# Taps of the last unit's first two tiles in two parts, and another order for the second half of the work

## The chip, the cores and the metric

One core of a Trainium2 chip. The metric is device time of the kernel in microseconds (us), the median of several executions; beside it stands one profiled execution, from which all durations come. The engines: TensorE (PE, its weight loads PEld), VectorE (DVE), ScalarE (ACT), GpSimd (POOL) and SyncE (SP, which issues loads).

## What is computed

Linear attention with a decaying state feeds a gated block:

```python
# q, k, v: (B=4, H=8, S=768, D=64)
for t in range(S):
    state = gamma * state + k[:, :, t] (outer) v[:, :, t]
    y[:, :, t] = scale * (q[:, :, t] @ state)
x = y.transpose(0, 2, 1, 3).reshape(B, S, 512)
gate = sigmoid(sum(conv_w[k] * x_shifted_by(4 - k) for k in range(5)))   # 5 taps along the sequence
out = (gate * (x @ w_val)) @ w_out
```

All inputs are float32, except the three weights of the block, which come in as float64.

## The kernel before

The sequence is cut into six chunks of 128 positions. A **unit** n (0 to 5) is one chunk with all four batches, 512 columns wide. Work on a unit comes in three kinds, which the code writes as letters of a string `WORK` (lines 60 to 64):

- `v`, a visit (`attention`, L896): the attention of one batch in one chunk, by 64x64 matmuls. It runs in two halves that TensorE may not interrupt (`hold`): `visit` (L502: outputs from the masked scores, L462; states, L446) and `rest_of_visit` (L514: outputs from the state, L462; scores of the next batch, L389). Between them ScalarE copies one column (`turn`, L512). In the last chunk the first half has no state matmuls of its own batch, and in the very last visit none at all. Afterwards VectorE masks the next scores (`mask`, L411) and writes the outputs into x (`evac`, L542); ScalarE rounds x (`round_x`, L552) and GpSimd takes the rest (`rest_x`, L557). GpSimd scales the next batch (`decay`, L378), ScalarE takes two copies of the state (`snap`, L457). A load for four batches ahead goes on SP's queue.
- `V`, a value tile (`val_tile`, L999; matmuls L680): 12 matmuls of 128x512, x times a quarter of w_val, in three passes (rounded x with both parts of the weight, rest of x with the rounded weight). With it comes `conv` (L973): the gate of that quarter, one tap on ScalarE (L662), four on VectorE (L664, each 128x512, accumulating in a PSUM tile `acc` of which there are two), and a sigmoid on ScalarE (L672). A tap reads all four batches, so the taps of a unit wait for the last visit of that unit. VectorE multiplies tile and gate (`gated`, L695).
- `O`, an output product. Units 1 to 4 use seven products of 12 matmuls of 128x256 each (`product_at`, L1067; L757), numbered 0 to 6 here, whose operands are sums and differences of quarters made on GpSimd (`g_sum`, L725; `g_low`, L742) and rounded on ScalarE (L738). Units 0 and 5 use four plain tiles (`out_tile`, L1098; L800).

Value tiles and products share two PSUM banks (`mm`): the products 0 and 2, 1 and 3, 4 and 6 share one bank each, so that bank stays taken from the first to the second of the pair. A new tile waits for the one two before it to be read out.

`WORK` gives each step a due time by adding up nominal durations. The function `plan` (L98) then orders all steps: each step gets a rank, its own due time or earlier if someone needs it earlier, and whenever an engine comes free, the ready step with the lowest rank is put next on that engine's queue, by fixed estimated durations. So the string gives an order of preference, not the order itself. The queues are in order on the chip: a step that isn't ready holds up what is queued behind it on its engine.

The last unit's end goes so: its fourth visit, evacuation, rounding, its taps, four value tiles, four output tiles, the last one in two halves.

Of the kernel before, what the change touches and what calls it, by code (L numbers as in the profile page):

```python
# [16 lines left out]
P = 128  # L17
HALF = 64
NPAIR = 4
TAPS = 5  # L20
# [24 lines left out]
TIMES = {  # L45
    "DVE": (0.69, 0.60),
    "tap": (0.76, 0.665),
    "ACT": (0.62, 0.525),
    "snap": (0.38, 0.28),
    "POOL": (1.29, 1.24),  # L50
    "decay": (1.05, 1.01),
}
# [6 lines left out]

WORK = (  # L60
    "spyzsyzsysyzwwzVVhwwvVVvOOOvOvvvVVvVVvTVOOVO"
    "VOvOvOvVvOVOOOVvOvOOVVvvOVOVOOOVVOOOvOvOvvOO"
    "OVOVVVOOOOO"
)

# [220 lines left out]
def tile_retention_gated_mlp(  # L286
# [10 lines left out]
    B, S, DM = out.shape  # L297
# [3 lines left out]
    NU = NCH  # L301
# [41 lines left out]
    def at(due, engine, cost, reads, writes, fn, *args):  # L343
        steps.append(Step(due, engine, cost, list(reads), list(writes), fn, args))
        return steps[-1]
# [6 lines left out]
    tiles, us, snaps, xs, xh, xl, decs, pos_ps = {}, {}, {}, {}, {}, {}, {0: base}, []  # L352
# [300 lines left out]
    accs, gvs, vps, ops, outs = {}, {}, {}, {}, {}  # L653
    gu, operands, banks, held = {}, {}, {}, {}

    def tap(n, m, k):
        x = xs[n][:, m]
        if k == 0:
            accs[n, m] = ps_a.tile([P, UT], F32, name="acc")
        acc = accs[n, m].rearrange("p (b t) -> p b t", t=P)  # L660
        if k == 0:
            nc.scalar.mul(acc, x[:, :, 0:P], cw_sb[:, m, 0:1])  # L662
        else:
            nc.vector.scalar_tensor_tensor(  # L664
                acc, x[:, :, k:k + P], cw_sb[:, m, k:k + 1], acc,
                op0=ALU.mult, op1=ALU.add,
            )
# [211 lines left out]
    def decay_at(t, g):  # L879
        at(t, "POOL", TIMES["decay"], ["small"], [("att", g % LB, "kn" if g < B else "vk")], decay, g)  # L880

    def scored_at(t, g):

        us_of[g] = Slot("u", 2)
        at(t, "DVE", TIMES["DVE"], [scored[g], "small"], [us_of[g]], mask, g)
        at(t + 0.01, "ACT", TIMES["snap"], ["z"], taken[g][1:], snap, g, 1)
# [9 lines left out]
    def attention(g, t):  # L896

        b, c = chunks[g]
        qk, vk = ("att", g % LB, "qk"), ("att", g % LB, "vk")
        u, y = us_of.pop(g), Slot("y", 1)  # L900
        n = 32
        if g + 1 < NG:
            decay_at(t - 0.01, g + 1)
            taken[g + 1] = [Slot("snap", 4), Slot("snap", 4)]
            at(t - 0.005, "ACT", TIMES["snap"], ["z"], taken[g + 1][0:1], snap, g + 1, 0)
            n += 16
        if c < NCH - 1:
            n += 16
        step = at(t, "PE", 1.0, [u, vk] + ([("att", (g + 1) % LB, "vk")] if g + 1 < NG else []), [y, "z"], visit, g)
        step.small = n  # L910
        step.turn = at(t + 0.5, "ACT", (0.25, 0.2), [y], ["turn"], turn, g)
        reads, writes = [qk, "turn"] + taken[g], [y]
        if g + 1 < NG:
            scored[g + 1] = Slot("sc", 1)
            reads.append(("att", (g + 1) % LB, "qk"))
            writes.append(scored[g + 1])
        step.hold = at(t + 1.0, "PE", 1.0, reads, writes, rest_of_visit, g)
        step.hold.small = 64 if g + 1 < NG else 32
        if g + 1 < NG:
            scored_at(t + 1.01, g + 1)  # L920
        if b == 0:
            xbufs[c] = Slot("x", XB)
            last = [xbufs[c - 1]] + [("x", c - 1, i) for i in range(B)]
            at(t + 0.5, "ACT", (0.25, 0.15), last, [xbufs[c]] + [("x", c, i) for i in range(B)], new_x, c)
        at(t + 1.9, "DVE", TIMES["DVE"], [y, ("dec", c % 2), xbufs[c]], [("x", c, b)], evac, g)
        if c + 1 < NCH:
            at(t + 2.4, "ACT", (0.4, 0.3), ["base", "small"], [("dec", (c + 1) % 2)], table, c + 1, b)
        split(c, b, t + 1.95)
        whole[c] = t + 2.0

    def convert(t, n):
        raw = wsts[n] if n != "cw" else "cwraw"
# [40 lines left out]
    def conv(n, m, t):  # L973
        acc = Slot("acc", 2)
        x = [xbufs[n]] + [("x", n, b) for b in range(B)]
        at(t, "ACT", (0.7, 0.62), x + ["cw"], [acc], tap, n, m, 0)
        for k in range(1, TAPS):
            at(t + 0.1 * k, "DVE", TIMES["tap"], x + ["cw"], [acc], tap, n, m, k)
        gates[n, m] = ("g", n, m)
        if m % 2 == 0:  # L980
            gslots[n, m // 2] = Slot("gate", GU)
        s = at(t + 0.5, "ACT", (0.6, 0.49), [acc], [gates[n, m]], sigmoid, n, m)
        if m % 2 == 0:
            s.writes += [gslots[n, m // 2], ("gopen", n, m // 2)]
        else:
            s.keeps.append(gslots[n, m // 2])
            s.reads.append(("gopen", n, m // 2))

    gslots, ops_of = {}, {}

    def split(n, b, t):
        if b == 0:
# [132 lines left out]
    for p, (kind, n) in enumerate(LOADS):  # L1125
        t = 0.1 * p
# [18 lines left out]
    t, whole = 6.0, {}  # L1145
# [3 lines left out]
    for what in WORK:  # L1149
        i = now[what]  # L1150
        now[what] += 1
        n, m = divmod(i, NPAIR)
# [4 lines left out]
        elif what == "s":  # L1157
            t = max(t, 6.0 + CHUNK * i)
# [27 lines left out]
        else:  # L1186
            n, m = products[i]
# [103 lines left out]
```

## Time and profile before

| | us |
|---|---|
| median of 3 runs (204.81 to 205.15) | 205.12 |
| the profiled execution | 205.91 |
| its span | 204.00 |
| TensorE busy | 195.1 (96%) |
| VectorE busy | 131.4 (64%) |
| ScalarE busy | 113.8 (56%) |
| GpSimd busy | 150.2 (74%) |

The span is the time from the first to the last recorded event; 1.91 us of the profiled execution lie around it. A visit appears as L462, L446, L462, L389 in TensorE's rows. Value matmuls (L680) and products (L757) stand between visits, partly interleaved one by one.

### The profile page before, as it was taken

Reading aid. Unit: us, or ns where it says so; the run is one execution under the profiler, and the core shown is the slowest. Engines: PE = TensorE matmul, PEld = TensorE weight load, DVE = VectorE, ACT = ScalarE, POOL = GpSimd, SP = SyncE. Lnnn points to the kernel's source line nnn. Section 1 sums busy time; section 2 is a strip of 40 time slices with the busy share of each in tenths; the row PEclk is TensorE's granted clock in tenths of the full one; section 3 lists DMA queues with packets and bytes.
Section 4 is the critical chain, followed back from the end, with each engine's and each line's share of the span. In section 5 each row is a group of like instructions: output and inputs, shape, how many; then the busy total and the mean of one; then the engine's idle time right before and its main releaser. Section 6 shows DMA issues by size and latency. Waiting matters only on the chain.

```text
span 204.0 us, 8170 instructions
## 1 busy us (share of the span) xinstructions
PE 195.1 (96%) x3640; PEld 164.3 (81%) x3640; DVE 131.4 (64%) x200; ACT 113.8 (56%) x245; POOL 150.2 (74%) x129
## 2 busy tenths in 40 slices
PE   8778999899998999999999999999999999999993
PEld 3456877778877888988988989988898998987882
DVE  1367799732878939994359995399922543999100
ACT  3476788935679468675138755247651535434221
POOL 0479999999989998999906999826995599222500
PEclk9999999999999999999999999999999999999998
DMA  6999998546846453364564472680010130220022
GB/s 199 371 416 416 408 421 297 214 180 223 286 159 249 181 209 154 111 234 141 208 177 175 140 286 82 261 274 3 3 51 0 55 109 0 103 78 28 0 103 103
DMA packets 11301, 36.25 MB, mean 178 GB/s; under 512 B 1154, under 2 KB 5634, under 8 KB 8708
## 3 DMA queue, kind: packets, MB, share of 16 engines
q1 hardware_dynamic: 5472, 29.43, 38.8%
q10 hardware_dynamic: 5796, 6.32, 9.2%
q8 instruction: 28, 0.46, 0.9%
q14 instruction: 5, 0.04, 0.1%
HBM read 29.46 MB, written 6.29 MB: 175 GB/s over the span
## 4 chain that ended last, share of the span: by engine, by line
PE 67%; DMA 4%; ACT 2%; DVE 0%; issue 0%; ACTq 0%
PE mm L680 27%; PE mm L757 20%; PE sy L462 8%; PE mm L800 6%; DMA out_dram<-o_sb 4%; PE sy L389 3%; PE z_ps L446 3%; ACT gate L672 0%; DVE top L787 0%; ACT snap L457 0%; ACT o_sb L813 0%; ACT acc L662 0%; ACT turned L512 0%; ACT gate L813 0%; ACT wst L646 0%
## 5 line engine op out<-in xcount | busy, mean ns | idle before, releaser
L664 DVE SCALAR_TENSOR_TENSOR acc<-x,cw_sb,acc 128x512 f32<-128x512 f32 x96 | 67.7, 750 | 4.4 <-ACT acc L662 3.8
L557 POOL TENSOR_TENSOR xl<-x,xh 128x512 fp32r<-128x512 f32 x24 | 31.2, 1301 | 11.2 <-ACT xh L552 11.2
L742 POOL TENSOR_TENSOR gvl<-gate,gvh 128x512 fp32r<-128x512 f32 x24 | 30.8, 1299 | 7.6 <-ACT gvh L738 7.6
L378 POOL TENSOR_TENSOR att<-att,small_sb 128x512 f32<-128x512 f32 x24 | 25.3, 1055 | 10.3 <-DMA att<-in_att_dram 10.2
L680 PE MATMUL mm<-xl,wvh 128*128 128x512 f32 x96 | 32.8, 398 | 0.0
L680 PE MATMUL mm<-xh,wvh 128*128 128x512 f32 x96 | 31.5, 405 | 0.4 <-ACT xh L552 0.4
L680 PE MATMUL mm<-xh,wvl 128*128 128x512 f32 x96 | 28.7, 397 | 0.0
L411 DVE TENSOR_TENSOR u<-sy,small_sb 128x512 f32<-128x512 f32 x20 | 13.7, 686 | 14.3 <-PE sy L389 8.9
L695 DVE TENSOR_TENSOR gate<-mm,gate 128x512 f32<-128x512 f32 x24 | 16.4, 685 | 8.9 <-PE mm L680 8.7
L672 ACT ACTIVATE gate<-acc 128x512 f32<-128x512 f32 x24 | 14.4, 603 | 13.7 <-DVE acc L664 12.2
L725 POOL TENSOR_TENSOR gate<-gate 128x512 f32<-128x512 f32 x16 | 20.6, 1293 | 0.5 <-DVE gate L695 0.4
L680 PEld LDWEIGHTS mm<-xl,wvh 128*128 128x128 f32 x96 | 17.9, 188 | 3.7
L680 PEld LDWEIGHTS mm<-xh,wvh 128*128 128x128 f32 x96 | 17.3, 188 | 4.4 <-ACT xh L552 0.6
L680 PEld LDWEIGHTS mm<-xh,wvl 128*128 128x128 f32 x96 | 17.7, 188 | 3.8
L552 ACT CAST xh<-x 128x512 fp32r<-128x512 f32 x24 | 14.8, 618 | 10.0 <-DVE x L542 9.6
L738 ACT CAST gvh<-gate 128x512 fp32r<-128x512 f32 x24 | 14.5, 620 | 9.5 <-DVE gate L695 5.3
L706 POOL TENSOR_TENSOR gvl<-gate,gvh 128x512 fp32r<-128x512 f32 x8 | 10.4, 1296 | 11.7 <-ACT gvh L702 11.7
L662 ACT ACTIVATE acc<-x,cw_sb 128x512 f32<-128x512 f32 x24 | 16.6, 694 | 3.7 <-DVE x L542 3.6
L542 DVE TENSOR_TENSOR x<-sy,dec 128x512 f32<-128x512 f32 x20 | 13.6, 682 | 7.5 <-ACT snap L457 3.2
L457 ACT COPY snap<-z_ps 128x256 f32<-128x256 f32 x40 | 14.1, 375 | 2.9 <-PE sy L462 1.7
L757 PE MATMUL mm<-wst,gvh 128*128 128x256 f32 x96 | 15.5, 282 | 0.0
L462 PEld LDWEIGHTS sy<-u,att 64*64 64x64 f32 x640 | 11.2, 134 | 5.3 <-issue 2.9
(78 smaller groups left out, 382.7 us busy)
## 6 DMA issues: line engine op xcount, KB each, us to landing
att<-in_att_dram SPq DMA_DIRECT2D x20, 1024.0 KB, 5.3
wst<-in_w_dram SPq DMA_DIRECT2D x8, 512.0 KB, 10.4
out_dram<-o_sb ACTq DMA_DIRECT2D x15, 256.0 KB, 2.9
att<-in_att_dram SPq DMA_DIRECT2D x3, 768.0 KB, 8.9
out_dram<-top ACTq DMA_DIRECT2D x8, 256.0 KB, 2.4
att<-in_att_dram SPq DMA_DIRECT2D x5, 256.0 KB, 5.5
att<-in_att_dram SPq DMA_DIRECT2D x1, 512.0 KB, 3.5
out_dram<-gate ACTq DMA_DIRECT2D x2, 128.0 KB, 1.7
```

The costliest lines, as they stand in the source:

```text
L378: nc.gpsimd.tensor_tensor(v, v, vd_sb[:, c, :].unsqueeze(2).broadcast_to([P, 8, HALF]), op=ALU.mult)
L462: nc.tensor.matmul(sy[cols, h, off:off + HALF], lhsT=lhsT, rhs=rhs, start=start, stop=True, skip_group_check=True,)
L552: nc.scalar.copy(xh[n][:, :, b], xs[n][:, :, b, HALO:])
L557: nc.gpsimd.tensor_tensor(xl[n][:, :, b], xs[n][:, :, b, HALO:], xh[n][:, :, b].bitcast(F32), op=ALU.subtract)
L662: nc.scalar.mul(acc, x[:, :, 0:P], cw_sb[:, m, 0:1])
L664: nc.vector.scalar_tensor_tensor(acc, x[:, :, k:k + P], cw_sb[:, m, k:k + 1], acc, op0=ALU.mult, op1=ALU.add,)
L680: nc.tensor.matmul(vps[n, m], lhsT=w[:, m, ct * P:(ct + 1) * P], rhs=xx[n][:, ct].rearrange("p b t -> p (b t)"), start=(i == 0), stop=(i = ...
L695: nc.vector.tensor_tensor(gv, vps.pop((n, m)), gv, op=ALU.mult)
L725: engine.tensor_tensor(block(n, k), block(n, a), block(n, b), op=getattr(ALU, op))
L738: nc.scalar.copy(g_part(n, k, 0), block(n, k))
L742: engine.tensor_tensor(low, block(n, k), operands[n, k, 0].bitcast(F32), op=ALU.subtract)
L757: nc.tensor.matmul(banks[bank][:, tt * 256:(tt + 1) * 256], lhsT=g[:, ct, tt * P:(tt + 1) * P], rhs=weight(w, part % 2)[:, ct], start=(k i ...
```

## The change

The taps of value tiles 0 and 1 of unit 5 are made in two parts. The first part covers batches 0 to 2 (384 of 512 columns) and becomes due right after the third visit of that unit; the second covers batch 3 (128 columns) and waits for the fourth. The ScalarE tap and the four VectorE taps each become two instructions, so ten instructions for these tiles become twenty. The other tiles keep whole taps. The middle line of `WORK` is another string with the same letters; the first three of its 44 letters stay. By units and batches (v4.2 is the visit of batch 2 in unit 4, V3.1 value tile 1 of unit 3, O2.5 product 5 of unit 2), from the first differing letter on, before:

```
O1.4 v3.1 O1.5 v3.2 V2.3 v3.3 O1.6 V3.0 O2.0 O2.1 O2.2 V3.1 v4.0 O2.3 v4.1 O2.4 O2.5 V3.2 V3.3 v4.2 v4.3
O2.6 V4.0 O3.0 V4.1 O3.1 O3.2 O3.3 V4.2 V4.3 O3.4 O3.5 O3.6 v5.0 O4.0 v5.1 O4.1 v5.2 v5.3
O4.2 O4.3 O4.4 V5.0 O4.5 V5.1 V5.2 V5.3 O4.6 O5.0 O5.1 O5.2 O5.3
```

and after:

```
v3.1 v3.2 O1.4 v3.3 O1.5 V2.3 V3.0 v4.0 V3.1 v4.1 O1.6 O2.0 O2.1 V3.2 O2.2 v4.2 v4.3
V3.3 O2.3 V4.0 O2.4 O2.5 V4.1 V4.2 O2.6 O3.0 O3.1 V4.3 O3.2 O3.3 O3.4 O3.5 O3.6 v5.0 O4.0 v5.1 O4.1 O4.2 O4.3 v5.2 v5.3
O4.4 V5.0 O4.5 V5.1 V5.2 V5.3 O4.6 O5.0 O5.1 O5.2 O5.3
```

```diff
--- before.py
+++ after.py
@@ -59,7 +59,7 @@
 
 WORK = (
     "spyzsyzsysyzwwzVVhwwvVVvOOOvOvvvVVvVVvTVOOVO"
-    "VOvOvOvVvOVOOOVvOvOOVVvvOVOVOOOVVOOOvOvOvvOO"
+    "VOvvvOvOVVvVvOOOVOvvVOVOOVVOOOVOOOOOvOvOOOvv"
     "OVOVVVOOOOO"
 )
 
@@ -653,11 +653,11 @@
     accs, gvs, vps, ops, outs = {}, {}, {}, {}, {}
     gu, operands, banks, held = {}, {}, {}, {}
 
-    def tap(n, m, k):
-        x = xs[n][:, m]
-        if k == 0:
+    def tap(n, m, k, b0=0, b1=B):
+        x = xs[n][:, m, b0:b1]
+        if k == 0 and b0 == 0:
             accs[n, m] = ps_a.tile([P, UT], F32, name="acc")
-        acc = accs[n, m].rearrange("p (b t) -> p b t", t=P)
+        acc = accs[n, m].rearrange("p (b t) -> p b t", t=P)[:, b0:b1]
         if k == 0:
             nc.scalar.mul(acc, x[:, :, 0:P], cw_sb[:, m, 0:1])
         else:
@@ -926,7 +926,7 @@
         if c + 1 < NCH:
             at(t + 2.4, "ACT", (0.4, 0.3), ["base", "small"], [("dec", (c + 1) % 2)], table, c + 1, b)
         split(c, b, t + 1.95)
-        whole[c] = t + 2.0
+        whole[c] = has_x[c, b] = t + 2.0
 
     def convert(t, n):
         raw = wsts[n] if n != "cw" else "cwraw"
@@ -973,9 +973,19 @@
     def conv(n, m, t):
         acc = Slot("acc", 2)
         x = [xbufs[n]] + [("x", n, b) for b in range(B)]
-        at(t, "ACT", (0.7, 0.62), x + ["cw"], [acc], tap, n, m, 0)
-        for k in range(1, TAPS):
-            at(t + 0.1 * k, "DVE", TIMES["tap"], x + ["cw"], [acc], tap, n, m, k)
+        if n == NU - 1 and m < 2:
+            t3 = min(t, has_x[n, 2] + 0.01)
+            x3, x1 = x[0:B] + ["cw"], [x[0], x[B], "cw"]
+            at(t3, "ACT", (0.56, 0.48), x3, [acc], tap, n, m, 0, 0, 3)
+            for k in range(1, TAPS):
+                at(t3 + 0.01 * k, "DVE", (0.61, 0.52), x3, [acc], tap, n, m, k, 0, 3)
+            at(t + 0.05, "ACT", (0.38, 0.3), x1, [acc], tap, n, m, 0, 3, 4)
+            for k in range(1, TAPS):
+                at(t + 0.1 * k, "DVE", (0.35, 0.26), x1, [acc], tap, n, m, k, 3, 4)
+        else:
+            at(t, "ACT", (0.7, 0.62), x + ["cw"], [acc], tap, n, m, 0)
+            for k in range(1, TAPS):
+                at(t + 0.1 * k, "DVE", TIMES["tap"], x + ["cw"], [acc], tap, n, m, k)
         gates[n, m] = ("g", n, m)
         if m % 2 == 0:
             gslots[n, m // 2] = Slot("gate", GU)
@@ -986,7 +996,7 @@
             s.keeps.append(gslots[n, m // 2])
             s.reads.append(("gopen", n, m // 2))
 
-    gslots, ops_of = {}, {}
+    gslots, ops_of, has_x = {}, {}, {}
 
     def split(n, b, t):
         if b == 0:
```

## Rows read from the trace of the kernel before

**Rows 1.** The page: busy us of each engine, share of the span.

```profile
PE 195.1 (96%) x3640; PEld 164.3 (81%) x3640; DVE 131.4 (64%) x200; ACT 113.8 (56%) x245; POOL 150.2 (74%) x129
```

**Rows 2.** Stages: length, engines' busy us, granted clock, DMA share, GB/s.

```profile
20.27:62.29 42.02, 40.89 (x951) 32.60 (x952) 28.90 (x45) 30.87 (x69) 41.44 (x36) 1.00 0.75 278
62.29:169.56 107.27, 107.09 (x2146) 94.77 (x2146) 76.16 (x116) 59.61 (x131) 87.77 (x74) 1.00 0.41 143
169.56:200.67 31.11, 30.77 (x228) 26.37 (x227) 16.85 (x26) 11.31 (x20) 9.90 (x8) 1.00 0.17 60
```

**Rows 3.** TensorE's waits after 62 us: total, times, longest.

```profile
PE sy L462 <- ACT turned L512: 0.8, 2, 0.5
```

**Rows 4.** TensorE by time, at 60.61: start, us, instructions, idle before.

```profile
58.79 1.20 PE L680 MATMUL mm<-xh,wvh 128*128 128x512 f32 x4
59.83 0.85 PE L680 MATMUL mm<-xh,wvl 128*128 128x512 f32 x3
60.61 0.69 PE L462 MATMUL sy<-u,att 64*64 64x64 f32 x32
...
62.29 0.69 PE L462 MATMUL sy<-att,snap 64*64 64x64 f32 x32 [0.52 <-ACT turned L512]
```

**Rows 5.** The same view around the last visit.

```profile
170.59 0.69 PE L462 MATMUL sy<-att,snap 64*64 64x64 f32 x32 [0.33 <-ACT turned L512]
171.21 0.62 PE L757 MATMUL mm<-wol,gvh 128*128 128x256 f32 x3
...
175.16 1.17 PE L680 MATMUL mm<-xh,wvh 128*128 128x512 f32 x4
...
176.63 0.64 PE L757 MATMUL mm<-woh,gvh 128*128 128x256 f32 x4
```

**Rows 6.** Chain that ended last: start, us, engine, line, instructions.

```profile
63.45 3.93 PE mm L680 x16
...
125.93 4.45 PE mm L757 x36
130.38 0.62 PE sy L462 x32
...
132.50 7.43 PE mm L680 x31
...
166.01 3.63 PE mm L757 x29
...
189.43 11.24 PE mm L800 x60
```

**Rows 7.** Groups by line: busy us, mean ns, idle before.

```profile
L664 DVE SCALAR_TENSOR_TENSOR acc<-x,cw_sb,acc 128x512 f32<-128x512 f32 x96 | 67.7, 750 | 4.4 <-ACT acc L662 3.8
...
L662 ACT ACTIVATE acc<-x,cw_sb 128x512 f32<-128x512 f32 x24 | 16.6, 694 | 3.7 <-DVE x L542 3.6
...
L423 DVE TENSOR_TENSOR xh<-small_sb 128x256 f32<-128x256 f32 x2 | 0.8, 422 | 3.5 <-DMA small_sb<-in_small_dram 3.5
```

**Rows 8.** Two stretches of 6 us, columns as in rows 2.

```profile
168.00:174.00 6.00, 5.67 (x101) 5.33 (x101) 2.48 (x4) 3.69 (x9) 5.00 (x5) 1.00 0.00 0
174.00:180.00 6.00, 6.00 (x40) 5.33 (x39) 5.86 (x10) 1.86 (x3) 1.29 (x1) 1.00 0.26 91
```

**Rows 9.** VectorE in order of time after the last visit.

```profile
171.42 0.69 DVE L542 TENSOR_TENSOR x<-sy,dec 128x512 f32<-128x512 f32 x1 [1.59 <-PE sy L462]
...
187.60 0.68 DVE L695 TENSOR_TENSOR gate<-mm,gate 128x512 f32<-128x512 f32 x1
189.53 0.69 DVE L695 TENSOR_TENSOR gate<-mm,gate 128x512 f32<-128x512 f32 x1 [1.25 <-PE mm L680]
```

**Rows 10.** ScalarE in order of time after the last visit.

```profile
172.15 0.69 ACT L662 ACTIVATE acc<-x,cw_sb 128x512 f32<-128x512 f32 x1 [1.61 <-DVE x L542]
...
173.35 0.62 ACT L552 CAST xh<-x 128x512 fp32r<-128x512 f32 x1
```


## The prediction

> **What bounds the kernel now.** I read the page's busy line first, then the busy time by stage, then the matmul engine's own waits, and last the chain that ended last. The busy line gives TensorE 195.1 of 204.0 us [rows 1], but the ends of matmuls are modelled, so that share alone proves nothing. The stages do: from 62.29 to 169.56 TensorE is busy 107.09 of 107.27 us, from there to its last matmul 30.77 of 31.11, all at a granted clock of 1.00 (the 2.4 GHz level), and only in the stage before it are 1.13 us idle (42.02 - 40.89) [rows 2]. After 62 us there are two waits that the trace can name, 0.8 us together, both in a visit, for the one-element copy on ScalarE (`turn`) [rows 3]; one of them (0.52) is the row at 62.29 itself and lies ahead of everything that the change reorders [rows 4], the other (0.33) is in the last visit [rows 5].
>
> Busy does not yet mean that the work can't go faster, so the pitch has to be looked at. 60 output matmuls take 11.24 us: 36 whole ones and 24 half ones, 0.233 and 0.118 us each (36 x 0.233 + 24 x 0.118 = 11.22). Ahead of a visit 36 product matmuls take 4.45 us, which is 36 x 0.118 = 4.25 and 0.2 for going over from and to the small matmuls; 31 value matmuls after it take 7.43, which is 31 x 0.233 = 7.22 and the same 0.2 [rows 6]. There are 14 such stretches after 63 us, from 63.45 to 166.01, and each exceeds matmuls x pitch by 0.16 to 0.23 us. So in the part that the change reorders the time is matmuls x pitch plus visits, and a visit costs 130.38 to 132.50 = 2.12 us plus that 0.2 [rows 6]. The end is set by the number of matmuls, not by their order.
>
> **The change part by part.** *The new order.* It holds the same letters: visits, value tiles and products are as many as before, and no matmul is added or taken away. Visits 2 and 3 of unit 3 move ahead of product 5 of unit 1, the visits of unit 4 ahead of some value tiles and products, and before the last visit stand two more products of unit 4: seven letters O stand behind the last v, nine before. That moves 2 x 12 x 0.118 = 2.83 us of TensorE from behind the last visit to ahead of it, and the sum on TensorE is zero. What can be gained is idle time only: 107.27 - 107.09 = 0.18 and 31.11 - 30.77 = 0.34 us [rows 2], and of the second 0.33 stay, since the last visit has no state matmuls between its two halves and nothing else may run there [rows 5]. So removal is worth 0 to 0.2 us; I take 0, since no row names a cause for the 0.18.
>
> What moves with a visit: a scaling on GpSimd (L378), one mask and one evacuation on VectorE, two snapshots on ScalarE, a load on SP's queue. GpSimd is busy 87.77 of 107.27 us in that stage, VectorE 76.16, ScalarE 59.61, and the DMA share is 0.41 [rows 2]; none is the bound, but each has stretches without a gap. Two adjacent visits need other work between them while the mask is made: the least between two visits in the trace is seven value matmuls, to the start of the next visit at 60.61 [rows 4]. The bulk work that covers that stays on hand, because visits moved forward leave products behind. I take 0 for it; the bounds are 0 and the 0.52 that the densest pair of the trace paid, when ScalarE's queue held up its `turn` [rows 4]. The two products that now precede the last visit bring a result copy and a send on ScalarE ahead of its `turn`; the same 0.52 bounds that.
>
> *The taps in two parts.* No row has a tap of 384 or 128 columns. On VectorE 128x256 took 422 ns (a two-operand product on SBUF) and the 512-wide tap 750 [rows 7]; the difference of 328 for 256 columns makes 1.28 ns a column, so 384 columns are about 0.59 us and 128 columns 0.26; with the fixed part of the tap kept larger, 0.35. I take 0.61 and 0.33. ScalarE's first tap took 694 ns [rows 7], and two parts of it take at most one whole more. For two tiles with four vector taps each, VectorE gets 8 x (0.61 + 0.33) = 7.5 us where it had 8 x 0.75 = 6.0, so 1.5 us more (bounds 0.8 and 1.7), and ScalarE at most 2 x 0.69 = 1.4 more, which it has: it is busy 3.69 and 1.86 of 6 us around the visit [rows 8]. But 8 x 0.61 of it lies ahead of the last visit, where VectorE is busy 2.48 of 6 us, and behind the visit it has 8 x 0.33 = 2.6 in place of 6.0 in a stretch where it is busy 5.86 of 6 [rows 8]. So the work that VectorE has left after the last batch falls by 3.4 us, against 2.83 us of cover that TensorE gives up.
>
> Whether these balance is what the tail hangs on. Now TensorE runs from 171.21 to its last value matmul without a gap, and the gatings of the last two tiles follow at 187.60 and 189.53, the latter as a wait for TensorE, not for the taps [rows 9]. So now there is a slack on the taps' side; afterwards it grows by some 0.5 us. The tail costs nothing more, and gains nothing, since it was not waiting.
>
> *A rule on instruction size.* In the tail VectorE has no gap to spare [rows 8], so more instructions there would count in full. The Trainium skill's page "Perfetto Trace Analysis", section "Optimizing Scalar/DVE Operations", says that each such instruction carries a fixed cost of its own (some 60 ns for VectorE on SBUF), that larger operations pay off where the engine is saturated, and that breaking them up can let work end sooner where it is not saturated but holds up another. By its figure the eight extra instructions would cost 0.5 us, an estimate; no run here shows a split tap. It speaks against the split in the tail and for it ahead of the last visit, and it is one of the rivals below.
>
> *Sum.* 204.00 us of span + 0 (order) + 0 (taps) = 204.0; with the 1.91 us around it the profiled execution gave 205.91, and the median of the runs is 205.12, 0.79 less. On the scale of the median: 205.1.
>
> **The rivals.** *A hole behind the last visit (slower).* The first value tile of unit 5 can't start until the last batch is evacuated and rounded: now 171.42 to 173.97, so 2.76 us after the visit's end at 171.21 [rows 5, 9, 10]. TensorE covers that today with 31 product matmuls up to 175.16. In the new order one product is due there (12 x 0.118 = 1.42 us); a second one can follow in its bank (it is the seventh, whose matmuls ran at 176.63, ahead of the sixth) and makes 2.83; the sixth can't, it needs another bank. Since visits 3 and 4 of the last unit now stand side by side, part of this is spent between them. If less than 1.6 us is left (the evacuation 0.2 + 0.69 and the rounding 0.62, with the rounding put first on ScalarE), TensorE stands still: at worst 2.76 - 1.42 = 1.3 us, mostly some 0.6. That gives 205.6 to 206.4. For it: the cover shrinks just there. Against it: the rounding can go ahead of the tap on ScalarE, which now precedes it [rows 10].
>
> *The early taps don't come early, or the fixed cost eats them (slower).* If the first parts are queued on VectorE behind the last evacuation, the tail has all the old taps and 2.83 us less cover. The slack against that is the 1.25 us that VectorE waits for TensorE ahead of the gating at 189.53 [rows 9], so 2.83 - 1.25 = 1.6 us are lost, or with the 1.5 us that the split adds 3.1: 206.7 to 208.2. Against it: VectorE has 3.5 us free in 168 to 174 [rows 8], and the parts need only three batches. That is also the case in which the change doesn't do what it says. The page's rule above belongs to it.
>
> *The idle time goes (faster).* All idle after 62.29 is 0.52 us [rows 2], and a shift of queue order that reached back to the wait at 62.29 would give another 0.52 [rows 4]. With most of both, 204.1 to 204.7. Against it: the first 47 letters of the order stay, and nothing ahead of some 80 us depends on the later ones.
>
> **How the numbers follow.** What a measurement of this kernel can tell from no change is about 0.2%, 0.41 us. The forecast, 204.8 to 205.5, gets 0.60: the stage is full and the work is the same. The hole behind the last visit gets 0.18, the taps that come too late 0.07, the idle time that goes 0.15. So faster 0.15, same 0.60, slower 0.25. The range goes from 204.5, inside the faster case, to 206.3, which takes in nearly all of the hole; what is left out is about a third of the faster case, most of the late taps and a little of the hole, 0.1 to 0.15.
>
> **What would show it.** Right: TensorE's busy time from about 62 us to its last matmul within 0.3 us of its length, 14 stretches that still exceed matmuls x pitch by 0.2, the last matmul at 200.7 within 0.3; first tap parts of 128x384 on VectorE before the last evacuation; VectorE's taps ending nearer to the last visit, but gated products still waiting for TensorE. The hole would show as a wait of the first value matmul of unit 5 for ScalarE's `xh`, with an idle time ahead of it. Late taps would show as value or output matmuls that wait for VectorE's gating. The prediction is wrong if TensorE's last matmul moves by over 0.4 us, or if the kernel is faster with TensorE's busy time after 62 us unchanged.

## The result: slower by 0.57 per cent, and most of it lies behind the last matmul

The changed kernel takes 206.12 us (median of 21 runs, 205.50 to 208.22), the kernel before, run beside it, 205.12: ratio 1.0057, 95% interval 1.0038 to 1.0077. That is about 1.0 us more. (The ratios in this document are not quotients of the medians beside them; the two can differ by up to some 0.2 per cent, and the intervals belong to the ratios.) The time is inside the range given above, but the likeliest case, no change, did not come; the kernel is slower, and not by the mechanism of either rival on that side. That it lies inside the range is luck: the upper end was put there for the hole behind the last visit, which did not come.

What surprised first is that TensorE does what was forecast. The page's busy line, and below it the same two stages as in [rows 2], of the changed kernel (length, then busy time of TensorE, its weight loads, VectorE, ScalarE, GpSimd, then clock, DMA share, GB/s):

```profile
PE 195.5 (96%) x3640; PEld 163.6 (80%) x3640; DVE 132.1 (65%) x208; ACT 113.3 (56%) x247; POOL 150.0 (74%) x129
```

```profile
62.29:169.56 107.27, 106.76 (x2173) 93.90 (x2165) 78.53 (x124) 59.60 (x133) 87.72 (x73) 1.00 0.40 143
169.56:200.67 31.11, 30.57 (x175) 26.22 (x173) 14.10 (x26) 10.40 (x20) 9.50 (x8) 1.00 0.17 61
```

The second of these windows ends 0.54 us behind the last matmul now, so 30.57 of 30.57 us are busy in it; the 0.51 us of idle time now lie in the first (0.18 and 0.34 before), since the last visit with its wait has moved there. TensorE's waits after 62 us, against the two of [rows 3]:

```profile
PE sy L462 <- ACT turned L512: 0.3, 1, 0.3
```

The profiled execution of the changed kernel even has the shorter span, 203.8 us against 204.0, and its last matmul ends at 200.13 us, that of before at 200.66. Two executions have to be laid side by side from a common point, though. Up to about 98 us TensorE runs the same list of instructions in both kernels; the eleventh copy to `turned` (the third visit of unit 3) is the last thing they have in common. It stands here in before and here in after (ScalarE in order of time: start, us, line, instruction, idle time before it):

```profile
94.33 0.15 ACT L512 COPY turned<-sy 64x2 f32<-64x2 f32 x1 [1.74 <-PE sy L462]
```

```profile
93.68 0.15 ACT L512 COPY turned<-sy 64x2 f32<-64x2 f32 x1 [1.76 <-PE sy L462]
```

From there to the end of the last matmul are 200.66 - 94.33 = 106.33 us before and 200.13 - 93.68 = 106.45 after: 0.12 us more for the whole new order and the split taps. This measure repeats well: five traces of the old order with whole taps and the tiles in their old place (before and four of the runs below) give 106.28 to 106.33, five of the changed kernel, four of them with instructions added in the ending, 106.43 to 106.52. The 0.65 us by which the common point itself differs are not the change's; over the traces of this study it falls between 93.1 and 95.1 us.

So the loss is to be looked for behind the last matmul. Of before, the last matmul and the last output copy on ScalarE:

```profile
200.38 0.27 PE L800 MATMUL mm<-woh,gvl 128*128 128x256 f32 x1
```

```profile
200.75 0.37 ACT L813 COPY gate<-mm 128x256 f32<-128x256 f32 x1 [0.57 <-PE mm L800]
```

Of after, the same, and the end of the chain that ended last:

```profile
199.85 0.27 PE L800 MATMUL mm<-woh,gvl 128*128 128x256 f32 x1
```

```profile
200.50 0.37 ACT L813 COPY gate<-mm 128x256 f32<-128x256 f32 x1 [0.85 <-PE mm L800]
```

```profile
188.90 11.24 PE mm L800 x60
200.18 0.32 issue
200.50 0.37 ACT gate L813
```

The copy waits for the last matmul in both, yet it starts 0.09 us behind its end in before and 0.37 in after, and the chain puts 0.32 us down to "issue": time in which the engine waited for nothing that the profile shows. Besides, the time of a run exceeds its span by 1.88 us before (median of the runs) and by 2.22 after.

### The profile page after: what moved, and what is told of

It is laid out like the page before. It is cut to its first block, busy times and chain, and to the rows that moved or that the text cites. A ratio compares the mean times of both kernels' runs of the same rounds, so it can differ in the third digit from the quotient of the medians.

```text
span 203.8 us, 8184 instructions
## 1 busy us (share of the span) xinstructions
PE 195.5 (96%) x3640; PEld 163.6 (80%) x3640; DVE 132.1 (65%) x208; ACT 113.3 (56%) x247; POOL 150.0 (74%) x129
## 4 chain that ended last, share of the span: by engine, by line
PE 80%; POOL 8%; DVE 4%; ACT 4%; issue 3%; ACTq 0%; POOLq 0%; DVEq 0%
PE mm L680 28%; PE mm L757 20%; PE sy L462 11%; PE mm L800 10%; PE sy L389 4%; PE z_ps L446 3%; DVE acc L664 3%; PE ye L825 2%; POOL wol L621 2%; POOL att L378 2%; POOL up L609 1%; ACT dec L529 1%; POOL x L609 1%; POOL xl L557 1%; DVE top L585 1%
## 5 line engine op out<-in xcount | busy, mean ns | idle before, releaser
L664 DVE SCALAR_TENSOR_TENSOR acc<-x,cw_sb,acc 128x512 f32<-128x512 f32 (+2 forms) x104 | 69.0, 708 | 2.8 <-ACT acc L662 2.2
L680 PE MATMUL mm<-xl,wvh 128*128 128x512 f32 x96 | 32.1, 399 | 0.0
L680 PE MATMUL mm<-xh,wvh 128*128 128x512 f32 x96 | 30.7, 403 | 0.4 <-ACT xh L552 0.4
L680 PE MATMUL mm<-xh,wvl 128*128 128x512 f32 x96 | 27.8, 397 | 0.0
L512 ACT COPY turned<-sy 64x2 f32<-64x2 f32 x20 | 3.1, 155 | 28.6 <-PE sy L462 28.5
L662 ACT ACTIVATE acc<-x,cw_sb 128x512 f32<-128x512 f32 (+2 forms) x26 | 16.9, 658 | 0.8 <-DVE x L542 0.8
L757 PE MATMUL mm<-wst,gvh 128*128 128x256 f32 x96 | 16.5, 282 | 0.0
```

The lines of the kernel that those rows point to most:

```text
L664: nc.vector.scalar_tensor_tensor(acc, x[:, :, k:k + P], cw_sb[:, m, k:k + 1], acc, op0=ALU.mult, op1=ALU.add,)
L680: nc.tensor.matmul(vps[n, m], lhsT=w[:, m, ct * P:(ct + 1) * P], rhs=xx[n][:, ct].rearrange("p b t -> p (b t)"), start=(i == 0), stop=(i = ...
L757: nc.tensor.matmul(banks[bank][:, tt * 256:(tt + 1) * 256], lhsT=g[:, ct, tt * P:(tt + 1) * P], rhs=weight(w, part % 2)[:, ct], start=(k i ...
```

## Three theories

1. *Boundaries in the engines' instruction streams.* An engine's instructions are brought in by transfers of their own. The page lists them as a queue: five packets in the span of before, six in that of after, of about 8 KB each.

```profile
q14 instruction: 5, 0.04, 0.1%
```

```profile
q14 instruction: 6, 0.05, 0.1%
```

At a certain place in the stream an engine would stand still for some 0.3 us. Where it would have waited anyway nothing is lost; among the last instructions of the kernel everything is. The change shifts these places: ScalarE has 319 instructions on record before and 325 after (semaphore instructions included, which the queries of the profile leave out), SyncE 78 and 81, GpSimd 197 and 196.
2. *The new order costs*, in a way that the last matmul's time in one trace doesn't show.
3. *The split taps cost.*

The tables below use one measure: **tail** is the time from the end of the last matmul to the end of the run, that is the rest of the span in the profiled execution plus the median of what the runs have outside it; for before 3.39 + 1.88 = 5.27 us, for after 3.65 + 2.22 = 5.87. **TensorE** is the time from the eleventh `turned` to the end of the last matmul, 106.33 and 106.45.

## The experiments

**One part of the change at a time.** The new order with whole taps:

```diff
-    "VOvOvOvVvOVOOOVvOvOOVVvvOVOVOOOVVOOOvOvOvvOO"
+    "VOvvvOvOVVvVvOOOVOvvVOVOOVVOOOVOOOOOvOvOOOvv"
```

> The new order of the work with whole taps. ScalarE's instruction stream is 2 shorter than in the changed kernel (its two extra first taps), so the last output copy comes two instructions earlier. Theory 1 (the loss sits at a boundary of ScalarE's instruction memory that the longer stream moved ahead of the last output copy): no late last copy, the gap between the last matmul's end and the copy back at 0.10 us; time within 0.3 us of the kernel before, 204.9 to 205.4. Theory 2 (the new order itself costs, by some idle time on TensorE that this one profile doesn't show): 0.7 to 1.2 us slower than before. Theory 3 (the split taps cost in the tail): as before, but then the split alone must be slower.

Measured: 205.90 us, ratio 1.0042 (1.0019 to 1.0065). TensorE 106.89, 0.56 more than before; tail 3.65 + 1.84 = 5.49. The last copy is back at 0.09 us, but the time misses what theory 1 gives and fits theory 2. Where TensorE loses the 0.56 us is not shown: the trace names no wait of it that before has not.

The split taps with the old order (the changed kernel with the first line of that diff):

> The taps in two parts with the old order of the work. ScalarE's stream ends 4 instructions earlier than in the changed kernel. Theory 1 (boundary ahead of the last copy): not slower than before by over 0.3 us, 204.9 to 205.4. Theory 2 (order): as before. Theory 3 (the eight and two more instructions cost in the tail): 0.5 to 1.0 us slower than before.

Measured: 206.09 us, ratio 1.0058 (1.0034 to 1.0082). TensorE 106.95, 0.62 more; tail 3.26 + 2.24 = 5.50. Here TensorE does stand still. Its waits after 62 us, and its instructions in order of time behind the last visit:

```profile
PE sy L462 <- ACT turned L512: 0.3, 1, 0.3
PE mm L680 <- DVE top L773: 0.3, 1, 0.3
```

```profile
172.50 1.21 PE L757 MATMUL mm<-wst,up 128*128 128x256 f32 x8
173.55 0.27 PE L757 MATMUL mm<-wst,gvl 128*128 128x256 f32 x1
173.66 0.63 PE L757 MATMUL mm<-wst,up 128*128 128x256 f32 x4
174.60 1.20 PE L680 MATMUL mm<-xh,wvh 128*128 128x512 f32 x4 [0.31 <-DVE top L773]
```

Four half matmuls take 0.47 us, so the stretch from 173.66 should end at 174.13, and the next one begins at 174.60. The value tile waits there for VectorE to read a product out, which it does at 173.86, behind six parts of taps that it runs from 171.09 on. The time fits theory 3 and misses theory 1. By these traces either part alone costs TensorE some 0.6 us, and the two together 0.12: in the changed kernel neither of the two costs remains, and each part needs the other.

**ScalarE's stream, with copies onto a new tile.** Copies of one element per partition on ScalarE, ahead of the first output copy of the last unit, onto a tile made for them: 20 in the changed kernel, six in the kernel before.

```diff
+    pad = const.tile([P, 1], F32, name="pad")
     def store(n, b, cs=slice(0, DM)):
+        if (n, b) == (NU - 1, 0):
+            for _ in range(20):
+                nc.scalar.copy(pad, zero)
```

> The changed kernel with 20 more one-column copies on ScalarE ahead of the first of the last unit's output copies, where ScalarE waits 2.3 us for TensorE; they write a scratch tile. Theory 1: the boundary now falls among these copies, where TensorE covers it, so although the kernel has more to do it gets faster than the changed kernel by 0.3 to 0.6 us, to 205.5 to 205.8, and the gap ahead of the last copy falls from 0.37 to 0.10 us. Theories 2 and 3: no gain, 206.0 to 206.4.

Measured: 206.71 us, ratio 1.0074 (1.0051 to 1.0097). The last copy came at 0.09 us as theory 1 has it, the tail was 5.61, but TensorE took about 107.6: the twenty copies held up a store, and TensorE had to wait for it.

```profile
PE mm L800 <- ACT o_sb L818: 1.4, 1, 1.4
PE sy L462 <- ACT turned L512: 0.3, 1, 0.3
```

> The kernel before with 6 such one-column copies at the same place, which makes ScalarE's stream just as long as the changed kernel's. Theory 1: slower than before by 0.3 to 0.6 us, 205.4 to 205.8, with 0.37 us from the last matmul's end to the last copy. Theories 2 and 3: as before, 205.0 to 205.3.

Measured: 204.98 us, ratio 0.9995 (0.9975 to 1.0015). The last copy came at 0.37 us and the tail was 5.52, yet the kernel was no slower: TensorE took 105.80, 0.53 less than before. From the common point on, its matmuls of 512 columns took 231.3 ns each on average, from start to start, where the kernel before has 233.1. The new tile had moved every tile behind it by 32 bytes. The experiment therefore had a second change in it, and both were tried apart from here on.

**The same without moving anything; two other streams.** The copies now go onto the tile of the first sigmoid, which exists anyway:

```diff
+            for _ in range(6):
+                nc.scalar.copy(held["sig"], zero)
```

> The kernel before with six copies of one element per partition on ScalarE ahead of the first output copy of the last unit, onto the tile that the first sigmoid already wrote, so that no operand moves to another address. ScalarE then has 325 recorded instructions, as the changed kernel has, and its last output copy is the 320th. Theory 1 (a boundary of ScalarE's instruction stream ahead of the last output copy): that copy starts 0.37 us behind the last matmul instead of 0.09, the time outside the span stays at 1.85, and the median is 0.28 us above the kernel before: ratio 1.0014. Theory 2 (the loss is all in the new order): no change, ratio 1.000. If the earlier run with six copies onto a new tile was as fast as before only because that tile moved the other operands, this one shows the 0.28 that was hidden there.

Measured: 205.57 us, ratio 1.0009 (0.9976 to 1.0041), so the time alone decides nothing. The trace shows the late copy: TensorE 106.29, the last copy 0.37 us behind the last matmul, tail 3.66 + 1.85 = 5.51. The end of the chain has the same row that the changed kernel has:

```profile
190.13 11.24 PE mm L800 x60
201.42 0.32 issue
201.74 0.37 ACT gate L816
```

Nine such copies on VectorE (`nc.vector.tensor_copy(held["sig"], zero)`) at the same place:

> The kernel before with nine copies of one element per partition on VectorE ahead of the last unit's first output copy, where VectorE has no other work; VectorE then has as many instructions as with the split taps. It asks whether the time outside the span, 1.85 us in the kernels with whole taps and 2.23 in those with split taps, goes with the length of VectorE's program. If so: 2.2 outside the span and a ratio of 1.0018 with an unchanged span. If the time outside the span goes with something else of the split (GpSimd's program, which is one instruction shorter there): 1.85 and a ratio of 1.000.

Measured: 205.12 us, ratio 0.9989 (0.9966 to 1.0011), 1.87 us outside the span: not VectorE's program.

One addition on GpSimd in the changed kernel (`nc.gpsimd.tensor_tensor(held["sig"], zero, zero, op=ALU.add)`):

> The changed kernel with one addition of one element per partition on GpSimd ahead of the last unit's first output copy, where GpSimd is idle; its program then has as many instructions as that of the kernel before. If the time outside the span goes with GpSimd's program: 1.85 us outside the span instead of 2.23, and a median 0.37 us below the changed kernel, 205.75, ratio 1.0038. If it goes with VectorE's program or with anything else of the split: 2.23 and the changed kernel's 206.1, ratio 1.0057.

Measured: 205.76 us, ratio 1.0022 (0.9998 to 1.0046), and 1.87 us outside the span instead of 2.22, with one instruction. But the span's rest behind the last matmul grew from 3.65 to 3.99, so the tail stayed, at 5.86. The time outside the span goes with GpSimd's program, and yet there was nothing to win: the pause had only moved over the edge of what is recorded.

The first sigmoid's tile two elements wide, to move the others:

> The kernel before with the first sigmoid's tile one element wider per partition, nothing else: no instruction is added, but the tiles behind it may come to lie at other addresses. If the shorter steps of the value matmuls in the two runs with added copies (231.3 and 230.6 ns instead of 233.1) came from the new tile's place: steps of 231 ns here too, some 0.5 us less in 214 such steps, ratio 0.9976. If they came from the added instructions: 233 ns and ratio 1.000.

Measured: 205.20 us, ratio 1.0005 (0.9974 to 1.0036), steps 233.1 ns. Nothing had moved, since the program lays tiles out in units of 32 bytes, so this one answers nothing.

**Taking the pauses away one by one.** Six copies on ScalarE in the changed kernel:

> The changed kernel with six copies of one element per partition on ScalarE ahead of the last unit's first output copy, onto the first sigmoid's tile (made eight elements wide, which moves nothing). Theory (boundary of ScalarE's instruction stream): the pause of 0.28 us moves from the last output copy to six instructions earlier in the stream, where ScalarE waits for TensorE anyway; the last copy starts 0.09 us behind the last matmul instead of 0.37, and from the last matmul to the end of the run 5.6 us are left instead of 5.87: 205.84 us, ratio 1.0043. Rival (the loss is in the new order or the split taps, the late copy is another wait): the last copy stays at 0.37, 206.1, ratio 1.0057.

Measured: 205.88 us, ratio 1.0038 (1.0013 to 1.0064). Last copy at 0.09 us, tail 3.37 + 2.22 = 5.59, as expected.

Eight loads of one element on SyncE's queue, behind the last eight chunk loads:

```diff
         nc.sync.dma_start(out=tiles[g][:, part], in_=src)
+        if g >= NG - 8:
+            k = 2 + g % 6
+            nc.sync.dma_start(out=held["sig"][:, k:k + 1], in_=small[:, 0:1])
```

> The changed kernel with eight loads of one element per partition on SyncE's queue, behind eight of the later chunk loads, into columns that nobody reads; SyncE's program is then seven instructions longer and ScalarE's and GpSimd's are as long as they were. Theory (a boundary of SyncE's stream lies in its closing instructions, since the new order gives it 81 recorded instructions instead of 78): the boundary then falls while SyncE waits for the last transfer, the closing step of SyncE that came at 3.31 us behind the last matmul comes at about 2.95, and the tail from the last matmul to the end is 5.6 us instead of 5.87: 205.84 us, ratio 1.0043. Rival (that late step is a wait for something else): the tail stays at 5.87, 206.1, ratio 1.0057.

Measured: 205.58 us, ratio 1.0016 (0.9990 to 1.0043), tail 3.35 + 2.24 = 5.59. The sum came as expected, and SyncE's late closing step went. But ScalarE had one instruction less on record than planned (324). Its 320th is then the issue of the last store, which waits for the last copy in any case; the copy starts at 0.09 us, the issue at 0.49 as in before, and no pause shows. In exchange the last transfer landed 0.27 us later than in the other kernels with the copy at 0.09 (SyncE's wait for it ends at 2.49 us instead of 2.22). That delay is not explained; an instruction packet of 8 KB lies in the middle of this store's packets, at 1.05 to 1.61 us.

Twelve additions on GpSimd in the kernel before:

> The kernel before with twelve additions of one element per partition on GpSimd ahead of the last unit's first output copy, where GpSimd is idle. Theory (each engine's stream has such boundaries; GpSimd's lies between its last two closing instructions, where the trace has 0.37 us of nothing): the boundary falls among the additions instead, the 0.37 goes, and from the last matmul to the end 4.9 us are left instead of 5.27: 204.75 us, ratio 0.9982, faster than the kernel before. Rival (the 0.37 is a fixed part of the ending): tail 5.27, ratio 1.000.

Measured: 205.09 us, ratio 0.9988 (0.9961 to 1.0016); tail 3.14 + 1.87 = 5.01 instead of 5.27. The pause went, and 0.26 us were won where 0.37 was expected: 0.06 of the 0.37 pass between these two semaphores in any case, and SyncE's closing waits took 0.05 longer. In the time of the runs this isn't to be seen.

All three in the changed kernel (six, thirteen, eight):

> The changed kernel with all three: six copies on ScalarE, thirteen additions on GpSimd, eight loads of one element on SyncE. Theory (the changed kernel's loss is three boundaries at its end that the kernel before shows in part or not at all): no pause in the ending, tail 4.95 us instead of 5.87, 205.2 us, ratio 1.0004; what is left of a loss against the kernel before with its own pause gone (204.75) is what the new order and the split taps cost on TensorE, 0.1 to 0.4 us. Rival (the loss is in order and taps): 206.1, ratio 1.0057.

Measured: 205.03 us, ratio 1.0004 (0.9975 to 1.0033); tail 3.14 + 1.79 = 4.93. The changed kernel is level with the kernel before once its ending has no pauses, and this interval does not meet that of the changed kernel itself (1.0038 to 1.0077). With one addition at a time the intervals overlap, so there the traces carry the argument. Its page has eight instruction packets in the span:

```profile
q14 instruction: 8, 0.07, 0.1%
```

These are the closing instructions, from the records of semaphore and drain instructions that the views above leave out, in us behind the end of the last matmul:

| | before | after | after, ScalarE +6 | after, SyncE +8 | before, GpSimd +12 | after, all three |
|---|---|---|---|---|---|---|
| instructions on record: ScalarE, SyncE, GpSimd | 319, 78, 197 | 325, 81, 196 | 331, 81, 196 | 324, 88, 196 | 319, 78, 209 | 330, 88, 209 |
| last output copy starts | 0.09 | **0.37** | 0.09 | 0.09 | 0.09 | 0.09 |
| SyncE's wait for the last transfer ends | 2.22 | 2.50 | 2.22 | 2.49 | 2.22 | 2.22 |
| GpSimd's last drain ends | 2.86 | 3.16 | 2.89 | 3.12 | 2.91 | 2.91 |
| SyncE's last drain ends | 2.64 | **3.44** | **3.16** | 2.91 | 2.70 | 2.69 |
| GpSimd's last semaphore but one ends | 2.92 | 3.48 | 3.20 | 3.19 | 2.97 | 2.97 |
| GpSimd's last semaphore starts | **3.28** | 3.54 | 3.26 | 3.25 | 3.03 | 3.03 |
| span ends | 3.39 | 3.65 | 3.37 | 3.35 | 3.14 | 3.14 |
| outside the span | 1.88 | **2.22** | **2.22** | **2.24** | 1.87 | 1.79 |
| tail | 5.27 | 5.87 | 5.59 | 5.59 | 5.01 | 4.93 |

A bold number has a pause in it. Wherever one shows, it stands ahead of the same instruction by count: ScalarE's 320th on record, SyncE's 80th, GpSimd's 197th. In before, ScalarE (319) and SyncE (78) are through before theirs comes, and GpSimd's 197th is its last. In after, ScalarE's 320th is the last output copy and SyncE's 80th its last drain, for which the others wait; GpSimd has 196, and its pause lies outside the span, where it costs as much as inside. This last is read from the runs, since the trace ends before it: 2.22 to 2.24 us lie outside the span in the five kernels where GpSimd has 196 instructions on record (after, split alone, 20 copies, ScalarE +6, SyncE +8), 1.84 to 1.90 in those where it has 197.

The packets of the instruction queue, from the records of the transfers in the traces, fit this. The last three start 3.97, 4.38 and 4.72 us behind the last matmul's end in before, and 1.25, 3.96 and 4.62 behind it in after. ScalarE's six copies alone bring one of the three to 2.63 us ahead of that end, SyncE's loads alone one to 15.3 ahead, GpSimd's additions alone one to 26.8 ahead; with all three additions they lie 28.2, 15.4 and 0.2 us ahead, and none is left. So each of the three engines has one such packet to come near the end. Two things stay open. Where a pause shows, the packet starts some 0.6 to 0.9 us behind the paused instruction, so what the engine waits for in the pause is not shown. And the count alone does not make a pause: with the twelve or thirteen additions GpSimd's 197th on record is one of them, it follows the one before as closely as the others do (0.08 us), and nothing shows.

The Trainium skill's page "Runtime: NRT & Kernel Launch", section "Instruction fetch mechanics", says that an engine's instructions are streamed in by blocks through a queue that its sequencer drives, and that the cost of crossing into a new block is "mostly hidden". The traces agree for the stretch from 62 us to the last matmul, where TensorE is idle for 0.51 us in all, 0.3 of it a wait with a name, and not for the ending: there 0.28 us showed in full ahead of the last copy.

**Where the operands lie.** The first sigmoid's tile nine elements wide, and 17 wide; no instruction is added, the chunk loads, value operands and gated tiles lie 32 or 64 bytes further in each partition, the weights stay.

```diff
-        sig = const.tile([P, 1], F32, name="sig")
-        nc.scalar.activation(sig, nc.const_aps.tensor(0.0, (P, 1), F32), AF.Sigmoid)
+        sig = const.tile([P, 9], F32, name="sig")
+        nc.scalar.activation(sig[:, 0:1], nc.const_aps.tensor(0.0, (P, 1), F32), AF.Sigmoid)
```

> The kernel before with the first sigmoid's tile nine elements wide, no instruction added: every tile allocated behind it lies 32 bytes further in each partition (the chunk loads, the value operands, the gated tiles), the weights ahead of it stay. Theory (the operands' place sets the matmuls' step): steps of the value matmuls of 231.3 ns instead of 233.1 as in the run with six copies onto a new tile, which moved the tiles by the same 32 bytes; about 0.5 us less from the fifth visit to the last matmul: 204.6 us, ratio 0.9976. Rival (the added copies did it): 233 ns, ratio 1.000.

Measured: 204.69 us against 205.24 of before beside it; ratio 0.9990 (0.9962 to 1.0017), which includes no change. TensorE 105.85, 0.48 less; matmuls of 512 columns every 231.3 ns, output matmuls of 256 columns every 115.9 ns instead of 118.1. Of its chain, the first 16 value matmuls behind 62 us and the 60 output matmuls, which take 3.93 and 11.24 us in [rows 6]:

```profile
62.89 3.89 PE mm L680 x16
...
188.39 11.19 PE mm L800 x60
```

> The same with the tile 17 elements wide: everything behind it lies 64 bytes further. If the place works by its remainder to 64 bytes, the steps are 233 ns again and the ratio 1.000; if by any move off the old place, 231 ns and 0.9976.

Measured: 205.12 us, ratio 0.9994 (0.9968 to 1.0019); TensorE 106.36, steps of 233.1 and 118.2 ns. Of its chain, the same:

```profile
63.67 3.93 PE mm L680 x16
...
189.63 11.27 PE mm L800 x60
```

By the traces the place of the operands alone does it, and a move by 64 bytes does nothing where a move by 32 does; the times of these two runs alone do not show it.

**Both kernels without pauses and at the better place.**

> The kernel before with the tile nine elements wide, and with twelve copies on ScalarE, twelve additions on GpSimd and eight loads of one element on SyncE, so that no pause of an instruction stream lies in its ending: tail 4.95 us instead of 5.27, and 0.5 us less by the place: 204.3 us, ratio 0.996, faster than both kernels. If the place does nothing: 204.8, ratio 0.9985.

Measured: 204.38 us, ratio 0.9961 (0.9934 to 0.9987); TensorE 105.82, tail 4.96. It is faster than the kernel before and than the changed one.

> The changed kernel with the same place and the same kinds of additions (six, thirteen, eight). If order and split taps cost 0.14 us on TensorE, as its traces say: 0.14 above the kernel before made the same way, 204.45 us, ratio 0.9967. If they cost the 0.4 that are left of the measured loss: 204.7, ratio 0.998.

Measured: 204.37 us, ratio 0.9962 (0.9941 to 0.9983); TensorE 105.92, tail 4.91. Without the endings the two kernels take the same time, 204.38 and 204.37; by the traces new order and split taps together cost TensorE 0.10 us here.

**The account.** For every kernel, the two terms read from its one trace, against before (106.33 and 5.27), and what the medians of the runs say. All in us:

| kernel | TensorE | tail | sum | measured |
|---|---|---|---|---|
| changed kernel | +0.12 | +0.60 | +0.72 | +1.00 |
| order alone | +0.56 | +0.22 | +0.78 | +0.82 |
| split alone | +0.62 | +0.23 | +0.85 | +1.01 |
| after, 20 copies on a new tile | +1.27 | +0.34 | +1.61 | +1.63 |
| before, 6 copies on a new tile | -0.53 | +0.25 | -0.28 | -0.10 |
| before, ScalarE +6 | -0.04 | +0.24 | +0.20 | +0.46 |
| before, VectorE +9 | -0.04 | +0.03 | -0.01 | +0.01 |
| after, GpSimd +1 | +0.12 | +0.59 | +0.71 | +0.65 |
| after, ScalarE +6 | +0.10 | +0.32 | +0.42 | +0.74 |
| after, SyncE +8 | +0.11 | +0.32 | +0.43 | +0.44 |
| before, GpSimd +12 | -0.04 | -0.26 | -0.30 | -0.05 |
| after, all three | +0.19 | -0.34 | -0.15 | -0.11 |
| before, 32 bytes further | -0.48 | -0.02 | -0.50 | -0.55 |
| before, 64 bytes further | +0.03 | -0.01 | +0.02 | -0.12 |
| before, no pauses, 32 bytes | -0.51 | -0.31 | -0.82 | -0.86 |
| after, no pauses, 32 bytes | -0.41 | -0.36 | -0.77 | -0.87 |

The sums follow the medians within 0.32 us, nine of the sixteen within 0.1; the intervals of the ratios are 0.4 to 0.7 us wide to either side, so the column on the right can't test a single tenth. What they leave for the changed kernel, 0.28 us, stays open: it is as large as for the kernel before with six copies on ScalarE or twelve additions on GpSimd, the stretch ahead of the common point wanders by more, and the changed kernel with one more GpSimd instruction, with the same tail and the same TensorE time, measured 0.65.

## Why the prediction was wrong, point by point

*TensorE is the bound, and its time is matmuls x pitch.* Right: from 62.29 us to the last matmul it is idle for 0.51 us (0.52 before), 106.45 against 106.33 us from the common point, the one named wait is that of the last visit. The criterion of the last matmul at 200.7 within 0.3 failed as it was put (200.13), and so did the 0.4 us of the last sentence (it came 0.53 earlier), because both were read from the start of the span and not from a common point; so measured it moved by 0.12, the other way.

*The taps.* The sizes of the parts were right, and their price came out at its upper bound:

```profile
L664 DVE SCALAR_TENSOR_TENSOR acc<-x,cw_sb,acc 128x512 f32<-128x512 f32 x88 | 61.9, 749 | 2.6 <-ACT acc L662 2.2
...
L664 DVE SCALAR_TENSOR_TENSOR acc<-x,cw_sb,acc 128x384 f32<-128x384 f32 x8 | 4.6, 611 | 0.0
L664 DVE SCALAR_TENSOR_TENSOR acc<-x,cw_sb,acc 128x128 f32<-128x128 f32 x8 | 2.7, 353 | 0.1
```

0.61 us was forecast for 384 columns and 0.33 for 128; 0.61 and 0.35 came. Eight taps in two parts are 8 x (0.611 + 0.353 - 0.749) = 1.7 us more of VectorE's time, where the prediction took 1.5 (bounds 0.8 and 1.7) and estimated 0.5 from a figure for operands in SBUF; the taps accumulate in PSUM. Five of the eight first parts (1 + 2 + 2) run ahead of the last evacuation, the row at 167.62; the row of six behind it holds the other three and three small parts. And the last gatings wait for TensorE, longer than the 1.25 us of [rows 9]:

```profile
163.81 0.61 DVE L664 SCALAR_TENSOR_TENSOR acc<-x,cw_sb,acc 128x384 f32<-128x384 f32 x1
...
164.93 1.14 DVE L664 SCALAR_TENSOR_TENSOR acc<-x,cw_sb,acc 128x384 f32<-128x384 f32 x2
...
166.58 1.14 DVE L664 SCALAR_TENSOR_TENSOR acc<-x,cw_sb,acc 128x384 f32<-128x384 f32 x2
167.62 0.68 DVE L542 TENSOR_TENSOR x<-sy,dec 128x512 f32<-128x512 f32 x1
168.22 2.58 DVE L664 SCALAR_TENSOR_TENSOR acc<-x,cw_sb,acc 128x384 f32<-128x384 f32 x6
...
186.91 0.69 DVE L695 TENSOR_TENSOR gate<-mm,gate 128x512 f32<-128x512 f32 x1 [2.18 <-PE mm L680]
189.01 0.69 DVE L695 TENSOR_TENSOR gate<-mm,gate 128x512 f32<-128x512 f32 x1 [1.41 <-PE mm L680]
```

*The new order at nothing.* Right for the two parts together, wrong for the order alone, which the prediction costed as zero by itself: it takes 0.56 us, and with the split taps most of it is gone.

*A hole behind the last visit.* It did not come, and the cover was misjudged: 60 product matmuls stand between the last visit and the first value tile of unit 5, 7.45 us (167.21 to 174.66) where the prediction reckoned with 1.42 to 2.83:

```profile
166.58 0.69 PE L462 MATMUL sy<-att,snap 64*64 64x64 f32 x32 [0.33 <-ACT turned L512]
167.21 0.74 PE L757 MATMUL mm<-woh,gvh 128*128 128x256 f32 x4
...
173.23 1.59 PE L757 MATMUL mm<-wst,up 128*128 128x256 f32 x12
174.66 1.09 PE L680 MATMUL mm<-xh,wvh 128*128 128x512 f32 x4
```

*Late taps, or a fixed cost that eats them.* Not seen in the changed kernel; the 0.31 us wait of the split with the old order is the nearest to it.

*The sum.* Here is the step that failed: "204.00 us of span + 0 (order) + 0 (taps) = 204.0; with the 1.91 us around it". The tail, what follows the last matmul inside and outside the span, was carried over as a constant and never looked at. It is not one: 5.27 us before, 5.87 after. Of the 0.60, 0.28 are the pause ahead of the last output copy and 0.26 what the pause ahead of SyncE's last drain passes on (GpSimd goes on 0.30 us behind its own drain there, 0.04 before). GpSimd's own has only moved: 0.30 us less inside the span, 0.34 more outside. Two sub-steps stand behind it. The instructions that split taps and new order add were counted by the time that they take, not by the place that they give the instructions behind them; semaphore instructions were not counted at all. And the prediction's last sentence, "wrong if TensorE's last matmul moves by over 0.4 us", tied the result to the last matmul and left no case in which the time changes behind it.

## What to carry to other kernels

Compare two traces from a common instruction, not from the start of the span, and split the time into three: up to that point, from there to the last instruction of the bound engine, and from there to the end of the run. Where the bound engine's part has hardly changed, read the ending, its semaphore and drain instructions too: an edit anywhere that adds or drops a few instructions on ScalarE, SyncE or GpSimd can move a pause of about 0.3 us into or out of the last microseconds (nine more on VectorE moved none, TensorE was not tried). For a measurement of a few tenths of a per cent that is a confound of the size of the effect, and so is any edit that moves tiles to other addresses; an added instruction should write to a tile that exists.

## What the runs showed of the hardware

A pause of some 0.3 us (0.28 on ScalarE, 0.30 on GpSimd, 0.37 on SyncE, of which 0.26 reached the chain) stands ahead of a fixed instruction of the engine's stream, counted from its beginning (ScalarE's 320th on record, SyncE's 80th, GpSimd's 197th), in every trace in which that instruction is the last output copy, a drain or a semaphore of the ending. Where it was the issue of a store, one of the added copies or additions, or a wait for another engine, no pause showed. What the engine waits for in it is not shown.

The step from one matmul to the next depends on where in a partition the operands lie: 233.1 ns for 512 columns at the old place, 231.3 with the tiles 32 bytes further, 233.1 with 64; for 256 columns of the output 118.1, 115.9 and 118.2. Over the 106 us from the common point this makes 0.48 us. Which of the moved tiles it is was not tried.
